# Storing and loading the second step's matrices in parts of 112 and 12 rows

## The chip, the core and the metric

The kernel runs on one core of a Trainium2 chip. The metric is the device time of one execution in microseconds. A core has TensorE (PE; its weight loads are listed as PEld), VectorE (DVE), ScalarE (ACT), GpSimd (POOL) and SyncE (SP). In this kernel all transfers between on-chip memory and DRAM are issued from SP's queue. They are carried out by 16 DMA engines.

## The reference

Two blocks follow one another. The first is a long convolution along the sequence, with a filter made by a small network, and the second a layer with a cosine gate:

```python
h_filt = (np.maximum(pos_emb @ w1, 0.0) @ w2) * np.exp(-0.01 * pos)[:, None]
u = x * v                                  # 4 x 12480 x 128
y = irfft(rfft(u, 2 * S) * rfft(h_filt, 2 * S)[None])[:, :S]
t = (x * y).reshape(4 * 12480, 128)
h = t @ moe_w_in                           # 128 x 2048
out = (h * np.cos(h)) @ moe_w_out          # 2048 x 128
```

All is float32.

## The kernel before

The convolution is done as a transform in two steps, as matrix products. The transform has N1 x N2 = 96 x 120 places. The first step (F1, `f1_units`) multiplies by a fixed matrix over the blocks. The second (F2) multiplies, for each of the 96 values k1, by a matrix w of its own, with KE = 124 rows and 120 columns. Then the result is multiplied with the filter's transform h, and two inverse steps (I1, I2) follow. There are four batches. In between, the rows that are ready go through the layer block ("moe"), 98 groups of 16 column blocks each.

The order of all work is written out by hand: `units` is a generator that makes one pass of a step for each `next`, and each engine carries out its own instructions in the order in which they were emitted. A pass j of a step has a `before` (loads or preparation, some passes ahead), an `mm` (matmuls) and an `after` (eviction and arithmetic, carried out during the next pass).

The second step exists in two forms, and each has 48 passes of two matrices.

- For batch 0 and the filter, `f2_both_units` runs alone on the core, with no layer work beside it. In `before`, `make_w` makes the two matrices of the next pass: ACT writes a scaled copy to PSUM (L328), and DVE adds the other term into the tile w (L330, three buffers). SP stores w to the DRAM tensor wd (L670). PE multiplies the filter's data (L490, or L493 in two halves) and the batch's data (L137). In `after`, ACT copies the filter's result into a tile h (L683, three buffers) and SP stores it to the DRAM tensor hd (L685). DVE makes two products with h (L506), and POOL combines them (L513). In the last pass a table cs is loaded as well (L672), which I1 uses.
- For batches 1 to 3, `f2_units` loads w from wd (L648) and h from hd (L650) two passes ahead, into three buffers each. It is interleaved with the layer's matmuls by the main loop.

Every row of a w tile is 960 bytes (two matrices of 120 numbers), and a row of an h tile is 2048 bytes with 120 rows.

After `f2_both_units` comes I1 (`i1_units`), whose matmuls need cs and the last results of L513. Then come I2 and, from about 300 us on, the layer.

Of the kernel before, what the change touches and what calls it, by code (L numbers as in the profile page):

```python
# [34 lines left out]
def kernel(  # L35
# [46 lines left out]
    nc = tc.nc  # L82
# [10 lines left out]
    KE = ODD + H  # L93
# [26 lines left out]
    wd = dram.tile([N1 // 2, KE, 2, N2], F32, name="wd")  # L120
# [192 lines left out]
    def last_tables(pool):  # L313
        rows = pool.tile([N1, 4, R], F32, name="rows")

        tw_t = pool.tile([N1, 2, N2], F32, name="tw_t")
        return rows, tw_t
# [18 lines left out]
    def make_w(w, k1, **how):  # L336


        turn(w, even[:, 0, :], even[:, 1, :], tw_w[:, 0, k1:k1 + 1], tw_w[:, 1, k1:k1 + 1],
             **how)  # L340
# [140 lines left out]
    def f2_mm(ps, w, k1, i, filt=False):  # L481


        k = k1 + i
        pi = ps[0:N2, :].rearrange("p (r b g i) -> p g r b i", r=2, g=2, i=2)[:, i]
        if not filt:
            mm(pi, w[:, i, :], parts[0:KE, :, k])
        elif k < KF:
            both = ftile[0:KE, :, k:k + N1 + 1:N1, :].rearrange("p b r i -> p r b i")
            nc.tensor.matmul(pi, w[:, i, :], both, start=True, stop=True)  # L490
        else:
            for r, src in enumerate((ftile[0:KE, :, k, :], above[0:KE, :, k - KF, :])):
                nc.tensor.matmul(pi[:, r], w[:, i, :], src, start=True, stop=True)  # L493

    def f2_product(pool, ps, h, k1, whole, engine=nc.gpsimd):


        y = parts[0:N2, :, k1:k1 + 2, :, :].rearrange("p r k b i -> p r b (k i)")
        t = pool.tile([N2, 2, CB, 4], F32, name="t", bufs=2)
        uu = ps[0:N2, :].rearrange("p (r b j) -> p r b j", r=2, j=4)  # L500
        if whole:
            for r, (dst, hh) in enumerate(((y, h[:, :, :, :]), (t[:, :, :, :], h[:, ::-1, :, :]))):
                u = uu[:, r]
                twice = bass.AP(tensor=u.tensor, offset=u.offset,
                                ap=[u.ap[0], [0, 2], *u.ap[1:]])
                nc.vector.tensor_tensor(dst, twice, hh, op=ALU.mult)  # L506
                yield
        for r, op in ((0, ALU.subtract), (1, ALU.add)):
            if not whole:
                nc.vector.tensor_tensor(y[:, r], uu[:, 0], h[:, r], op=ALU.mult)  # L510
                yield
                nc.vector.tensor_tensor(t[:, r], uu[:, 1], h[:, 1 - r], op=ALU.mult)  # L512
            (engine if r else nc.gpsimd).tensor_tensor(y[:, r], y[:, r], t[:, r], op=op)  # L513
            yield
# [59 lines left out]
    def units(n, steps, before, mm, after, parts, ahead=2, skip=0):  # L574


        for j in range(min(ahead, n)):
            for _ in before(j) or ():
                pass
        yield 0.0  # L580
        last = iter(())
        for j in range(n):
            early = iter(before(j + ahead) or () if j + ahead < n else ())
            now = None
            for i in range(parts):
                if i == skip or 2 * (i - skip) == max(parts, 2):
                    now = mm(j, now, int(i > skip))
                if i == 0 and parts == 1:
                    now = mm(j, now, 1)
                next(last, None)  # L590
                next(early, None)
                yield steps / parts
            for _ in early:
                pass
            next(last, None)
            last = after(j, now)
        for _ in last:
            pass
        yield REST
# [33 lines left out]
    def f1_units(bank, u, share, evict=f1_evict):  # L633
# [5 lines left out]

        return units(CB, F1_STEPS, lambda j: None, mm, lambda j, ps: evict(ps, j, share(j)), 2)  # L640

    def f2_units(bank):
        with tc.tile_pool(name="there", bufs=3) as pool:
            ws, hs = {}, {}

            def before(j):
                ws[j] = pool.tile([KE, 2, N2], F32, name="w")
                nc.sync.dma_start(ws[j][:, :, :], wd[j, :, :, :])  # L648
                hs[j] = pool.tile([N2, 2, CB, 4], F32, name="h")
                nc.sync.dma_start(hs[j][:, :, :, :], hd[j, :, :, :, :])  # L650

            def mm(j, ps, i):
                if i == 0:
                    ps = bank()
                f2_mm(ps, ws[j], 2 * j, i)
                return ps

            yield from units(N1 // 2, F2_STEPS, before, mm,
                             lambda j, ps: f2_product(pool, ps, hs.pop(j), 2 * j, False), 4)

    def f2_both_units(bank):

        with tc.tile_pool(name="both", bufs=2) as pool:
            ws = {}

            def before(j):
                ws[j] = pool.tile([KE, 2, N2], F32, name="w", bufs=3)
                for i in range(2):
                    make_w(ws[j][:, i, :], 2 * j + i, half=bank)
                nc.sync.dma_start(wd[j, :, :, :], ws[j][:, :, :])  # L670
                if j == N1 // 2 - 1:
                    nc.sync.dma_start(cs[:, :, :], csd[:, :, :])  # L672

            def mm(j, ps, i):
                if i == 0:
                    ps = bank(), bank()
                for k in range(2):
                    f2_mm(ps[1 - i], ws[j], 2 * j, k, filt=i == 0)
                return ps

            def after(j, ps):
                h = pool.tile([N2, 2, CB, 4], F32, name="h", bufs=3)
                nc.scalar.activation(h[:, :, :, :].rearrange("p r b j -> p (r b j)"),  # L683
                                     ps[1][0:N2, :], AF.Copy, scale=1.0 / M)
                nc.sync.dma_start(hd[j, :, :, :, :], h[:, :, :, :])  # L685
                last = j == N1 // 2 - 1
                yield from f2_product(pool, ps[0], h, 2 * j, not last,
                                      nc.vector if last else nc.gpsimd)

            yield from units(N1 // 2, F2_STEPS, before, mm, after, 4, ahead=1)  # L690
# [79 lines left out]
    def forward_units(bank, back):  # L770

        f2 = f2_units(bank)
        next(f2)
        yield from f1_units(bank, slots[0:R, :, :, :], lambda b: 1.0)
        yield from f2
        next(back)
        yield from i1_units(bank)
# [120 lines left out]
    with tc.manual_schedule():  # L898
        with tc.tile_pool(name="psum", bufs=8, space=PSUM) as psum, \
                ExitStack() as first:  # L900
            def bank():
                return psum.tile([P, BANK], F32, name="ps")
# [110 lines left out]
            rows, tw_t = last_tables(wpool)  # L1013
# [127 lines left out]
```

## Time and profile before

| what | value |
|---|---|
| median of three runs | 3636.73 us (3636.14 to 3637.93) |
| the profiled execution | 3637.09 us, of which its span is 3635.3 |
| granted TensorE clock, mean | 0.998 |
| PE busy | 3575.0 us (98%) |
| DVE busy | 2833.6 us (78%) |
| POOL busy | 2745.5 us (76%) |
| ACT busy | 2230.6 us (61%) |
| DMA, share of 16 engines (SP's queue) | 26.5%, 275 MB |
| stores of w (wd<-w) | 48 of 116.2 KB |
| loads of w (w<-wd) | 144 of 116.2 KB |
| stores of h, loads of h | 48 and 144 of 240 KB |

The profile records one execution. Its time is 1.8 us more than the span from the first to the last instruction. In lists of waits the numbers are the total in us, how many times, and the longest. In a timeline they are the start, the duration in us, and in brackets how long the engine was idle before and what ended that. In the tables by stretch of time each engine has its busy time and, in brackets, its number of instructions; behind them are the granted clock, the share of the DMA engines and GB/s. The rows of the DMA view that begin with "DMA" and digits cut the window into 40 slices and give the busy share of the 16 engines in tenths.

### The profile page before, as it was taken

Reading aid. Unit: us, or ns where it says so; the run is one execution under the profiler, and the core shown is the slowest. Engines: PE = TensorE matmul, PEld = TensorE weight load, DVE = VectorE, ACT = ScalarE, POOL = GpSimd, SP = SyncE. Lnnn points to the kernel's source line nnn. Section 1 sums busy time; section 2 is a strip of 40 time slices with the busy share of each in tenths; the row PEclk is TensorE's granted clock in tenths of the full one; section 3 lists DMA queues with packets and bytes.
Section 4 is the critical chain, followed back from the end, with each engine's and each line's share of the span. In section 5 each row is a group of like instructions: output and inputs, shape, how many; then the busy total and the mean of one; then the engine's idle time right before and its main releaser. Section 6 shows DMA issues by size and latency. Waiting matters only on the chain.

```text
span 3635.3 us, 101879 instructions
## 1 busy us (share of the span) xinstructions
PE 3575.0 (98%) x40826; PEld 2559.2 (70%) x40826; DVE 2833.6 (78%) x5289; ACT 2230.6 (61%) x4482; POOL 2745.5 (76%) x3237
## 2 busy tenths in 40 slices
PE   8999999999999999999999999999999999999999
PEld 7877767666678776666677776766667776666666
DVE  7877885688887886688887786578887667777877
ACT  7657666666554556656655556665655446666676
POOL 7767996688864896688864887588885558878777
PEclk9999999999999999999999999999999999999999
DMA  7444540022213550022211562022220350000000
GB/s 188 142 151 140 169 131 21 25 68 75 71 43 107 165 146 27 23 74 73 68 37 53 168 171 63 13 61 69 70 71 16 102 159 19 19 25 19 19 25 14
DMA packets 219584, 281.80 MB, mean 78 GB/s; under 512 B 18778, under 2 KB 156514, under 8 KB 218986
## 3 DMA queue, kind: packets, MB, share of 16 engines
q1 hardware_dynamic: 219114, 275.29, 26.5%
q8 instruction: 325, 5.32, 0.6%
q14 instruction: 145, 1.19, 0.1%
HBM read 194.75 MB, written 80.46 MB: 76 GB/s over the span
## 4 chain that ended last, share of the span: by engine, by line
PE 83%; DVE 5%; POOL 2%; ACT 1%; issue 1%; DMA 0%; SPq 0%; ACTq 0%; POOLq 0%; DVEq 0%
PE ph L137 30%; PE accb L846 17%; PE cv L137 17%; PE acca L846 13%; PE cv L457 3%; DVE gt L815 2%; DVE gt L821 2%; PE ph L141 1%; PE cv L141 1%; ACT gt L814 1%; POOL ts L829 1%; POOL slots L449 0%; POOL ts L832 0%; DVE t L512 0%; DVE slots L510 0%
## 5 line engine op out<-in xcount | busy, mean ns | idle before, releaser
L814 ACT ACTIVATE gt<-ph 128x512 int32<-128x512 f32 (+1 forms) x1380 | 821.9, 596 | 1083.5 <-PE ph L137 1029.0
L815 DVE SCALAR_TENSOR_TENSOR gt<-ph,gt 128x512 f32<-128x512 f32 (+1 forms) x1380 | 947.8, 687 | 666.1 <-ACT gt L814 661.9
L137 PE MATMUL ph<-at,w_in_sb 128*64 128x512 f32 (+1 forms) x5520 | 1432.0, 592 | 12.8 <-DVE gt L821 11.8
L829 POOL TENSOR_TENSOR ts<-gt 128x512 f32<-128x512 f32 (+2 forms) x784 | 998.9, 1274 | 569.7 <-PE accb L846 566.1
L820 ACT ACTIVATE gt<-gt 128x512 f32<-128x512 f32 (+1 forms) x1568 | 972.5, 620 | 5.9 <-DVE gt L815 4.7
L821 DVE TENSOR_TENSOR gt<-ph,gt 128x512 f32<-128x512 f32 (+1 forms) x1380 | 934.8, 677 | 0.0
L846 PE MATMUL accb<-ts,w_out_sb 128*64 128x128 f32 (+2 forms) x9408 | 653.4, 272 | 0.0
L832 POOL TENSOR_TENSOR ts<-ts,gt 128x256 f32<-128x256 f32 (+2 forms) x784 | 574.6, 733 | 61.5
L833 POOL TENSOR_TENSOR ts<-gt,ts 128x256 f32<-128x256 f32 (+2 forms) x784 | 573.5, 732 | 61.5
L846 PEld LDWEIGHTS acca<-gt,w_out_sb 128*64 128x64 f32 x6272 | 403.4, 136 | 256.3 <-issue 227.4
L846 PEld LDWEIGHTS accb<-ts,w_out_sb 128*64 128x64 f32 x9408 | 547.3, 137 | 0.0
L846 PE MATMUL acca<-gt,w_out_sb 128*64 128x128 f32 (+2 forms) x6272 | 481.9, 272 | 0.0
L846 PEld LDWEIGHTS accb<-gt,w_out_sb 128*64 128x64 f32 x3136 | 228.0, 136 | 245.4 <-issue 197.4
L137 PEld LDWEIGHTS ph<-at,w_in_sb 128*64 128x64 f32 x5520 | 360.1, 137 | 31.2 <-PE cv L141 11.3
L513 POOL TENSOR_TENSOR slots<-slots,t 120x256 f32<-120x256 f32 x383 | 277.5, 731 | 116.1 <-DVE t L512 63.0
L846 PE MATMUL accb<-gt,w_out_sb 128*64 128x128 f32 (+1 forms) x3136 | 314.3, 273 | 4.6 <-DVE ot L867 3.1
L846 PE MATMUL acca<-ts,w_out_sb 128*64 128x128 f32 (+1 forms) x3136 | 311.8, 272 | 2.6 <-POOL ts L832 2.3
L137 PEld LDWEIGHTS cv<-slots,tm 96*40 96x40 f32 (+1 forms) x3840 | 227.2, 125 | 121.4 <-issue 115.7
L137 PE MATMUL cv<-slots,tm 96*40 96x128 f32 (+1 forms) x3840 | 254.3, 273 | 4.3 <-DVE slots L535 3.4
L137 PEld LDWEIGHTS cv<-even,slots 120*64 120x64 f32 (+1 forms) x3072 | 168.3, 125 | 60.4 <-issue 58.2
L846 PEld LDWEIGHTS acca<-ts,w_out_sb 128*64 128x64 f32 x3136 | 204.4, 137 | 4.5 <-POOL ts L832 4.3
L137 PEld LDWEIGHTS cv<-slots,w 124*64 124x64 f32 (+1 forms) x1152 | 89.1, 134 | 154.1 <-issue 144.0
(136 smaller groups left out, 3875.2 us busy)
## 6 DMA issues: line engine op xcount, KB each, us to landing
h<-hd SPq DMA_DIRECT2D x144, 240.0 KB
tm<-td SPq DMA_DIRECT2D x96, 312.0 KB
xt<-in_x_dram SPq DMA_DIRECT2D x120, 208.0 KB
xs<-in_x_dram SPq DMA_DIRECT2D x120, 208.0 KB
zd<-xs SPq DMA_DIRECT2D x119, 208.0 KB
tile<-zd SPq DMA_DIRECT2D x96, 256.0 KB
vt<-in_v_dram SPq DMA_DIRECT2D x90, 208.0 KB
w<-wd SPq DMA_DIRECT2D x144, 116.2 KB
```

What stands on the lines that cost most here:

```text
L137: nc.tensor.matmul(dst[lo:hi], left[:, lo:hi], right, start=start, stop=stop)
L141: nc.tensor.transpose(dst, src, ident[0:n, 0:n])
L457: nc.tensor.matmul(dst[lo:hi], u[:, b, lo:hi, i], c1[0:u.shape[0], r:r + 2, :].rearrange("p r k -> p (r k)"), start=True, stop=True)
L513: (engine if r else nc.gpsimd).tensor_tensor(y[:, r], y[:, r], t[:, r], op=op)
L814: nc.scalar.activation(turns, ph[:, 0:m], AF.Identity, bias=phase)
L815: nc.vector.scalar_tensor_tensor(out=part, in0=ph[:, 0:m], scalar=phase, in1=turns, op0=ALU.add, op1=ALU.subtract)
L820: nc.scalar.activation(part, part, AF.Sin, scale=scale)
L821: nc.vector.tensor_tensor(part, ph, part, op=ALU.mult)
L829: nc.gpsimd.tensor_tensor(ts[:, 0:2, 0:half], gt[:, :, half:2 * half], gt[:, 0, 0:2 * half].rearrange("p (h n) -> p h n", h=2), op=ALU.sub ...
L832: nc.gpsimd.tensor_tensor(t[2], t[1], b11, op=ALU.add)
L833: nc.gpsimd.tensor_tensor(t[3], b21, t[2], op=ALU.subtract)
L846: nc.tensor.matmul(acc[h * CB:(h + 1) * CB, place, 0:r], w_out_sb[:, pair, weight, :], right[:, h * r:(h + 1) * r], start=(pair == 0 and i ...
```

## The change

A tuple of two slices cuts the 124 rows of w into the first 112 and the last 12. The store of w and the load of w are each issued as two transfers, one for each slice, to and from the same places. Nothing else differs: the same tiles and buffers, the same matmuls, the same order of everything else.

```diff
+    parted = slice(0, KE // 16 * 16), slice(KE // 16 * 16, KE)
+
     def f2_units(bank):
...
             def before(j):
                 ws[j] = pool.tile([KE, 2, N2], F32, name="w")
-                nc.sync.dma_start(ws[j][:, :, :], wd[j, :, :, :])
+                for rows in parted:
+                    nc.sync.dma_start(ws[j][rows, :, :], wd[j, rows, :, :])
                 hs[j] = pool.tile([N2, 2, CB, 4], F32, name="h")
                 nc.sync.dma_start(hs[j][:, :, :, :], hd[j, :, :, :, :])
...
                 for i in range(2):
                     make_w(ws[j][:, i, :], 2 * j + i, half=bank)
-                nc.sync.dma_start(wd[j, :, :, :], ws[j][:, :, :])
+                for rows in parted:
+                    nc.sync.dma_start(wd[j, rows, :, :], ws[j][rows, :, :])
                 if j == N1 // 2 - 1:
                     nc.sync.dma_start(cs[:, :, :], csd[:, :, :])
```

## The prediction

> **What bounds the kernel now.** I read the page first, then the windows, the waits and the timeline of the two stages that the diff touches, and last the DMA view of single transfers.
>
> ```profile
> span 3635.3 us, 101879 instructions
> PE 3575.0 (98%) x40826; PEld 2559.2 (70%) x40826; DVE 2833.6 (78%) x5289; ACT 2230.6 (61%) x4482; POOL 2745.5 (76%) x3237
> PE 83%; DVE 5%; POOL 2%; ACT 1%; issue 1%; DMA 0%; SPq 0%; ACTq 0%; POOLq 0%; DVEq 0%
> ```
>
> TensorE sets the end nearly everywhere and DMA has 0% of the chain. The chain is a share of the whole span, though. The stores of w lie in one stage, about 137 to 238 us; its waits say something else.
>
> ```profile
> ACT h L683 <- DMA hd<-h: 34.4, 41, 1.7
> DVE slots L506 <- ACT h L683: 12.5, 41, 1.1
> PEld ps L493 <- PE ps L137: 11.2, 22, 1.3
> ```
>
> 41 of the 48 passes wait for a store of h to land, because h has three buffers. DVE then waits for ACT, and PE for both. What that does to the pace is read from the starts of one kind of matmul; busy time does not show it, since the page models matmul ends.
>
> ```profile
> 141.43 1.03 PE L490 MATMUL ps<-ftile,w 124*120 124x256 f32 x4
> 143.17 1.03 PE L490 MATMUL ps<-ftile,w 124*120 124x256 f32 x4
> 144.67 0.60 ACT L683 ACTIVATE h<-ps 120x512 f32<-120x512 f32 x1 [1.04 <-DMA hd<-h]
> 144.90 1.03 PE L490 MATMUL ps<-ftile,w 124*120 124x256 f32 x4
> ...
> 201.09 0.60 ACT L683 ACTIVATE h<-ps 120x512 f32<-120x512 f32 x1 [0.74 <-DMA hd<-h]
> 203.11 0.60 ACT L683 ACTIVATE h<-ps 120x512 f32<-120x512 f32 x1 [0.74 <-DMA hd<-h]
> 205.13 0.60 ACT L683 ACTIVATE h<-ps 120x512 f32<-120x512 f32 x1 [0.74 <-DMA hd<-h]
> ```
>
> Until the first wait a pass takes 1.735 us (141.43 to 144.90 is two passes), PE back to back. Afterwards it takes 2.02. From the pass at 139.70 to the last at 232.77 there are 46 passes: 93.1 us, mean 2.023.
>
> Why does the store of h land late? The first DMA line and packet count below are of a window with one load of w alone (710.4 to 716 us), the second count of one load of 128 rows alone (570.8 to 575), the third of the store stage (137 to 238).
>
> ```profile
> DMA  0000000290200022222220000000000000000000
> DMA packets 128, 0.12 MB, mean 21 GB/s; under 512 B 4, under 2 KB 128, under 8 KB 128
> DMA packets 145, 0.28 MB, mean 66 GB/s; under 512 B 16, under 2 KB 16, under 8 KB 144
> DMA packets 12666, 17.57 MB, mean 174 GB/s; under 512 B 911, under 2 KB 6983, under 8 KB 12656
> ```
>
> A load of w is 124 packets of a row and 4 small ones, and keeps 2 tenths of the 16 engines busy for 1.3 us: four engines carry it, 31 rows each. The transfer of 128 rows closes with 16 small packets. In the store stage 48 x (4 + 15) = 912 fit the 911: w on 4 engines, h on 15. The trace's completion records say the same and give the pattern for other row counts: 96 and 128 rows 16 engines, 120 rows 15, 104 rows 13, 124 rows 4, always the largest divisor up to 16. They also show the store of h issued at 201.85: eleven completions by 3.23 us after issue, the last four at 4.67 to 5.24. Single packets take 44 ns (960 B row of w) and 84 ns (2048 B row of h) in the median, so a pass loads the shared four engines with 31 x 44 + 8 x 84 = 2.04 us. That is the 2.02 us period. These four engines bound the stage.
>
> **The change, part by part.**
>
> *Stores.* 112 rows should go to 16 engines (7 rows each) and 12 rows to 12 (one each), an estimate from the divisor pattern above. The fullest engine then has 8 x 44 + 8 x 84 = 1.02 us a pass; with the mean packet times of the stage (47 and 119 ns) 1.33. Both lie under 1.735, so this bound goes. What is late next:
> - PE needs 1.735 a pass.
> - DVE: starts at 199.70, 200.31, 200.91 and two w products 0.25 apart, 1.71; its new wait for a second store may add one more 21 ns wait instruction of L330, 1.73.
> - The loop through the three h buffers: ACT 0.60, the wait for SP 0.2 plus 0.4 for the new issue ahead of it, landing 3.2 plus 8 x 0.047 for the added rows, over three passes: 4.8 / 3 = 1.6.
> - SP: w issues cost 0.24 us (4 engines) and transfers on 13 to 16 engines 0.31 to 0.38, so 0.35 + 0.31 + 0.37 = 1.03.
>
> PE and DVE are within 0.03 of each other, and PSUM banks couple them; I take 1.75, bounds 1.735 and 1.85. Gain 46 x (2.023 - 1.75) = 12.6 us, bounds 13.3 and 8.0.
>
> *End of the stage.* The last data matmuls start at 233.75 and the next step at 238.48, released by POOL. In these 4.73 us ACT waits for h twice more. Without that DVE does the two products of pass 46 in 1.21 us, and POOL's three L513 follow as now (236.08 to 238.48, 2.40). That is 3.61, a gain of 1.1. The load of cs sits behind one more issue on SP (0.35 us); its completions on the free engines came 2.1 us after issue, so it stays ahead.
>
> *Clock.* The PE gap there shrinks from 3.71 to 2.6 us.
>
> ```profile
> 243.00:244.00 1.00, 1.00 (x7) 1.00 (x7) 0.14 (x1) 0.32 (x1) 0.00 (x0) 0.50 1.02 418
> 245.00:246.00 1.00, 1.00 (x12) 1.00 (x11) 0.00 (x0) 0.67 (x2) 0.35 (x1) 1.00 0.96 343
> 548.00:550.00 2.00, 1.02 (x5) 0.63 (x7) 0.59 (x1) 0.00 (x0) 1.92 (x4) 0.60 0.00 0
> ```
>
> The seventh column is granted clock: 0.50 until 244.62 (the trace's clock records: 6.83 us from 237.79), which costs the matmuls from 238.48 on 3.07 us. After a gap of 2.35 us (546.63 to 548.98) it also fell, for 3.41 us. So a gap of 2.6 may cost nothing, one such stretch (1.7) or the same as now. I take a gain of 1.3, bounds 0 and 3.1. The Trainium skill ("TensorE: Matmul & The Clock Gate", Part 1: The HAM clock gate) has the clock drop after at least one idle window of about 3.4 us; by it 2.6 us would cost nothing and the sum would be 1.8 us lower. The drop at 548.40 came after 1.77 us of idle, so here the trace is harsher than the rule.
>
> *Loads.* 144 loads become 288. No wait for w shows in those three passes, the DMA share there is 0.15 to 0.27, and a load is issued two passes ahead. SP gets 144 x 0.35 us more, in stretches in which it mostly waits for buffers; queued behind it are the h loads, the loads of the layer's tiles and output stores. PE must wait for one more completion per pass: at most 144 x 51 ns (the wait instructions of L137 there) = 7.3 us, if matmuls do not cover it. They do now: at 705.26 and 705.37 two of them run while matmuls from 705.25 to 706.29 are under way. I take 0 and keep 7.3 for the range. A gain is excluded, as nothing waits for these loads.
>
> Sum against the profiled execution: 3637.1 - 12.6 - 1.1 - 1.3 = 3622.1. The median is 0.4 lower, so 3621.7. All that follows the stage is PE-bound and moves forward with it. A comparison of this kernel can tell about 0.2%, 7.3 us.
>
> **Rivals.**
>
> *A. The parts share one limit.* If the write path as a whole held the stage at its 171 to 186 GB/s, spreading rows would change nothing: 3637. For it: the rate is steady over 90 us. Against it: with h alone in the queue 234 to 235 us shows 251 GB/s, and eleven of fifteen completions are early. The Trainium skill ("DMA: Bandwidth & Descriptors", Rules for kernel authors) speaks for A: two transfers to disjoint partitions go one after the other on the same engines, so one should not bother. It supposes that the undivided transfer sprays over all 16; this one has 4. Chance 0.05.
>
> *B. The parts are not spread*, 28 and 3 rows on the same four engines: the same 31 x 44 ns, 3637. Against it: the divisor pattern over five row counts. 0.03.
>
> *C. Another loop steps in at once*, such as the h loop or the banks, with a period near 1.90: 46 x 0.12 + 1.1 = 6.6 us, 3630. For it: landing would need 4.1 us instead of 3.6. 0.05.
>
> *D. Slower: SP becomes the bound.* Three issues a pass decide once they average more than 2.02 / 3 = 0.67 us. A full queue stretches an issue: that of h at 145.62 took 1.13. At 0.75 each a pass takes 2.25, 46 x 0.23 = 10.6 us longer, 3647. Against it: the median of h is 0.378, and those stretched stand where the four engines were backlogged. 0.05.
>
> **How the numbers follow.** My forecast has the remaining 0.82, at 3621.7. Its own range runs from 3617 (1.735 a pass, no clock loss there, and none at 548, where the drop costs half of 548.98 to 551.82, 1.4: 18.9 us in all) to 3630 (1.80 a pass, no clock gain and half of the 7.3). That holds C as well and leaves out A, B, D and the outermost corners. Faster by over 0.2%: 0.82 and a little of C, 0.84. Within 0.2%: A, B, the rest of C and the corner where every PE wait counts, 0.11. Slower: D, 0.05.
>
> **What would show it.** Right: no ACT wait for hd<-h after the first passes, L490 and L493 starts 1.74 to 1.8 us apart, the i1 matmuls starting near 225 us, and 48 x (16 + 12 + 15) small packets in the store stage. Wrong: a period still near 2.02 (A, B), SP issues of w above 0.6 us (D), ACT still waiting for hd<-h at about 1.9 (C), or PE gaps ahead of the first w matmuls from 705 us on.

## The result and the profile after

The changed kernel takes 3617.86 us in the median of six runs (3617.44 to 3621.77), the kernel before 3636.13 (3633.47 to 3637.93). The ratio is 0.9953, with an interval of 0.994 to 0.9966: 17 us less by the ratio, 18 by the medians. The profiled execution after took 3621.77 us (span 3620.0), 15.3 less than the one before. It is the longest of the six, and why comes out below.

The page of after, its first lines:

```profile
span 3620.0 us, 102190 instructions
PE 3565.4 (98%) x40826; PEld 2560.2 (71%) x40826; DVE 2830.0 (78%) x5289; ACT 2228.6 (62%) x4482; POOL 2749.6 (76%) x3237
```

The same matmuls, fewer busy microseconds, and the same 98%: the share says nothing about what was won. The waits of the store stage do (137 to 224 us of after; the lines of `f2_both_units` have moved by 4, so L683 is L687):

```profile
ACT h L687 <- PE ps L493: 11.6, 20, 0.6
ACT h L687 <- PE ps L490: 11.3, 19, 0.6
...
ACT h L687 <- DMA hd<-h: 4.3, 5, 1.4
```

Of 41 waits for a store of h five are left, 4.3 us instead of 34.4. The prediction had expected none after the first passes; these are later. Each follows an issue on SP that took unusually long: a store of h issued at 170.33 took 1.81 us, and ACT waited at 174.37, 175.98 and 177.40; parts of w issued at 204.62 and 218.52 took 0.98 and 1.06 us, and ACT waited at 207.12 and 221.12. Otherwise ACT now waits for PE, which is the other way round from before. The timeline of after shows the pace from the start of the stage and late in it:

```profile
139.66 1.03 PE L490 MATMUL ps<-ftile,w 124*120 124x256 f32 x4
141.39 1.03 PE L490 MATMUL ps<-ftile,w 124*120 124x256 f32 x4
143.13 1.03 PE L490 MATMUL ps<-ftile,w 124*120 124x256 f32 x4
144.86 1.03 PE L490 MATMUL ps<-ftile,w 124*120 124x256 f32 x4
...
201.22 0.74 SPq L674 DMA_DIRECT2D wd<-w  x2
201.66 0.60 ACT L687 ACTIVATE h<-ps 120x512 f32<-120x512 f32 x1 [0.61 <-PE ps L493]
202.06 0.32 SPq L689 DMA_DIRECT2D hd<-h  x1
...
203.41 0.60 ACT L687 ACTIVATE h<-ps 120x512 f32<-120x512 f32 x1 [0.61 <-PE ps L493]
```

The 1.735 us of the first passes now lasts; from 201.66 to 203.41 a pass takes 1.75. From ACT's sixth h to its 41st the mean is 1.744 us, against 2.048 before. PE waits for nobody between 140 and 219 us. DVE has hardly more room, as the stretch 175 to 185 us shows, before and after (PE, PEld, DVE, ACT and POOL in this order):

```profile
175.00:185.00 10.00, 9.79 (x59) 7.44 (x58) 8.84 (x21) 6.14 (x16) 6.95 (x10) 1.00 0.63 186
```

```profile
175.00:185.00 10.00, 10.00 (x70) 9.13 (x70) 10.00 (x24) 6.99 (x20) 7.90 (x13) 1.00 0.78 228
```

The DMA view of 137 to 224 us counts the small packets that close each engine's share:

```profile
DMA packets 13899, 17.72 MB, mean 204 GB/s; under 512 B 2070, under 2 KB 8142, under 8 KB 13889
```

48 x (16 + 12 + 15) = 2064, and the load of cs closes with up to 15 more. So 112 rows went to 16 engines and 12 rows to 12. The completion records (the times at which each engine reports its share of a transfer as landed) of after put the part issued at 201.22 at 1.64 to 2.06 us after its issue, the small part at 1.48 to 1.79, and the store of h issued at 202.06 at 2.05 to 2.47, with no late group of four.

### The profile page after: what moved, and what is told of

Same layout as the page of the kernel before. It is cut to its first block, busy times and chain, and to the rows that moved or that the text cites. A ratio compares the mean times of both kernels' runs of the same rounds, so it can differ in the third digit from the quotient of the medians.

```text
span 3620.0 us, 102190 instructions
## 1 busy us (share of the span) xinstructions
PE 3565.4 (98%) x40826; PEld 2560.2 (71%) x40826; DVE 2830.0 (78%) x5289; ACT 2228.6 (62%) x4482; POOL 2749.6 (76%) x3237
## 4 chain that ended last, share of the span: by engine, by line
PE 83%; DVE 5%; POOL 2%; ACT 1%; issue 1%; DMA 0%; ACTq 0%; POOLq 0%; DVEq 0%; SPq 0%
PE ph L137 30%; PE accb L850 17%; PE cv L137 17%; PE acca L850 13%; PE cv L457 3%; DVE gt L825 2%; DVE gt L819 2%; PE ph L141 1%; PE cv L141 1%; POOL ts L833 1%; ACT gt L818 1%; POOL slots L449 0%; POOL ts L836 0%; DVE t L512 0%; DVE slots L510 0%
## 5 line engine op out<-in xcount | busy, mean ns | idle before, releaser
L137 PE MATMUL ph<-at,w_in_sb 128*64 128x512 f32 (+1 forms) x5520 | 1432.9, 592 | 12.9 <-DVE gt L825 11.9
L137 PEld LDWEIGHTS ph<-at,w_in_sb 128*64 128x64 f32 x5520 | 359.9, 137 | 31.4 <-PE cv L141 11.3
L137 PEld LDWEIGHTS cv<-slots,tm 96*40 96x40 f32 (+1 forms) x3840 | 227.7, 125 | 120.7 <-issue 116.0
L137 PE MATMUL cv<-slots,tm 96*40 96x128 f32 (+1 forms) x3840 | 254.5, 273 | 4.1 <-DVE slots L535 3.4
L137 PEld LDWEIGHTS cv<-even,slots 120*64 120x64 f32 (+1 forms) x3072 | 167.8, 125 | 61.1 <-issue 57.8
L137 PEld LDWEIGHTS cv<-slots,w 124*56 124x56 f32 (+1 forms) x1152 | 89.1, 134 | 154.1 <-issue 143.9
```

The lines of the kernel that those rows point to most:

```text
L137: nc.tensor.matmul(dst[lo:hi], left[:, lo:hi], right, start=start, stop=stop)
```

## The experiments

Theory T is that of the prediction: four engines carried all of w and bounded the store stage, and nothing waited for the loads. The rivals were that the loads count (L), that PE's added waits cost time (W), that the write path as a whole is the limit (A), that smaller parts help whatever their rows (P), and that SP's issues become the bound (D).

**Only the stores, and only the loads.** The first kernel leaves the load in `f2_units` whole, the second leaves the store in `f2_both_units` whole:

```diff
 # stores alone: in f2_units
-                for rows in parted:
-                    nc.sync.dma_start(ws[j][rows, :, :], wd[j, rows, :, :])
+                nc.sync.dma_start(ws[j][:, :, :], wd[j, :, :, :])
 # loads alone: in f2_both_units
-                for rows in parted:
-                    nc.sync.dma_start(wd[j, rows, :, :], ws[j][rows, :, :])
+                nc.sync.dma_start(wd[j, :, :, :], ws[j][:, :, :])
```

> Only the stores of w are issued in parts of 112 and 12 rows; the loads stay whole. Theory T (the four engines that carry w bound the store stage, and nothing waits for the loads): the whole gain is here, about 3618 us, with the passes of the store stage 1.735 us apart and the i1 matmuls starting near 224 us. Rival L (a good part of the gain comes from the loads in the three later passes, which leave four engines free for other transfers): 3625 or more. Rival W (the second completion that PE waits for in each load costs time): below 3618, down to 3611.

> Only the loads of w are issued in parts; the stores stay whole. Theory T: no change, 3636 us within 2 us, the store stage with its 2.02 us a pass. Rival L: faster by several us. Rival W: slower by up to 7 us (144 x 51 ns).

Stores alone: 3616.53 us (3616.15 to 3621.18), ratio 0.9952 (0.9939 to 0.9964), all of the gain. Loads alone: 3634.29, ratio 0.9999 (0.999 to 1.0008), none. The waits of the kernel with only the loads in parts, 137 to 238 us:

```profile
ACT h L686 <- DMA hd<-h: 36.0, 43, 1.7
```

The old wait is all there. Of L and W the interval leaves room for no more than 0.1%, 3.6 us. The added PE waits exist: over the same piece of work (705.3 to 1015.3 us before, 690 to 1000 after) the wait instructions of L137 grow from 141 to 176. PE's busy time does not, 305.89 and 305.90 of 310 us. Matmuls cover them in this stretch.

**Smaller parts on fewer engines.** Against the kernel with only the stores in parts:

```diff
-    parted = slice(0, KE // 16 * 16), slice(KE // 16 * 16, KE)
+    parted = slice(0, KE // 2), slice(KE // 2, KE)
```

> The stores of w are issued in two parts of 62 rows each; loads whole. Both parts are smaller than the whole, but by the divisor pattern 62 rows go to 2 engines each. Theory T: the two fullest engines carry 62 x 44 + 8 x 84 ns = 3.4 us a pass, so the store stage grows by 46 x (3.4 - 2.02) = 63 us against the kernel before, to about 3700 us. Rival A (the write path as a whole is the limit, the rows' place on engines does not matter): 3636. Rival P (two smaller transfers help whatever their rows): 3618.

Measured 3699.38 us (3698.95 to 3701.21), ratio 1.0176 (1.016 to 1.0191): 64 us slower than the kernel before, where T had said 63. The sum hit so closely in part by luck: in the profiled executions the 46 passes took 59.6 us more, since the first of them still ran faster, and 4.4 us came from the end of the stage, which the sum had left out. The DMA view and the waits, 137 to 300 us:

```profile
DMA packets 12676, 17.60 MB, mean 108 GB/s; under 512 B 907, under 2 KB 6975, under 8 KB 12666
```

```profile
ACT h L686 <- DMA hd<-h: 105.2, 45, 3.9
```

48 x (2 + 2 + 15) = 912 small packets fit the 907: each 62 rows went to two engines. The same bytes as before move at 108 GB/s instead of 174, and a pass takes 3.413 us, where 62 x 44 + 8 x 84 ns is 3.40. The completion records of the store of h issued at 200.67 have 13 engines at 3.58 us or sooner and the last two at 8.05 and 8.10. P and A cannot give this.

**One part, with a row count that divides well.** The tiles are made 128 rows high, and four computed rows are stored and loaded that no matmul uses:

```diff
-    wd = dram.tile([N1 // 2, KE, 2, N2], F32, name="wd")
+    wd = dram.tile([N1 // 2, P, 2, N2], F32, name="wd")
-    even = const.tile([KE, 2, N2], F32, name="even")
+    even = const.tile([P, 2, N2], F32, name="even")
...
-            mm(pi, w[:, i, :], parts[0:KE, :, k])
+            mm(pi, w[0:KE, i, :], parts[0:KE, :, k])
```

> The tiles w and wd get 128 rows (four more rows are computed, stored and loaded, and never used by a matmul); each store and load is one transfer of 128 rows, 120 KB. Theory T: 128 rows go to 16 engines, 8 rows each, so the fullest engine has 8 x 44 + 8 x 84 ns as with 112 and 12, and the time is that of the changed kernel, 3618 us within 2, although there is one transfer again and 3% more bytes. Rival P (the gain needs two parts): 3636.

3619.12 us (3616.03 to 3619.98), ratio 0.9954 (0.9941 to 0.9966). The DMA view from 137 to 224 us:

```profile
DMA packets 13533, 17.92 MB, mean 206 GB/s; under 512 B 1502, under 2 KB 7766, under 8 KB 13523
```

The 1502 small packets are 48 x (16 + 15) + 15 less one. One transfer with more bytes does as well as two: the spread over engines is what counts, not the parting.

**Five parts.** With the engines loaded as in the change, again against the kernel with only the stores in parts:

```diff
-    parted = slice(0, KE // 16 * 16), slice(KE // 16 * 16, KE)
+    parted = [slice(r, r + 32) for r in (0, 32, 64)] + [slice(96, 112), slice(112, KE)]
```

> The stores of w are issued in five parts of 32, 32, 32, 16 and 12 rows (16, 16, 16, 16 and 12 engines), so the load of the engines stays that of 112 and 12 rows; loads whole. SP then issues six transfers in a pass. Rival D put the point from which SP decides at the issues of a pass adding up to more than the pass. At the 0.31 to 0.38 us of the page's issues, 5 x 0.34 + 0.37 = 2.1 us a pass, so 46 x (2.1 - 1.735) = 17 us more than with two parts: about 3634 us, with SP issuing without a break. If SP's issue is free beside everything else: 3617. If stretched issues of 0.75 us are the rule with many in flight: 4.1 us a pass, 3720.

3667.83 us (3667.59 to 3668.16), ratio 1.0091 (1.0077 to 1.0105): SP decides, as D says, but far more than expected. SP's own waits in 137 to 225 us come first, and then its issues of two passes from the timeline:

```profile
SPq L688 <- ACT h L686: 1.5, 4, 0.5
SPq L673 <- DVE w L330: 1.5, 1, 1.5
SPq L688 <- ACT ps L328: 0.3, 1, 0.3
```

```profile
201.49 2.92 SPq L673 DMA_DIRECT2D wd<-w  x5
204.50 0.32 SPq L688 DMA_DIRECT2D hd<-h  x1
204.92 2.15 SPq L673 DMA_DIRECT2D wd<-w  x5
207.17 0.32 SPq L688 DMA_DIRECT2D hd<-h  x1
```

SP hardly waits for anyone. Five issues of w take 2.15 us, or 2.92 where one of them is stretched (the trace has it at 1.17), and h another 0.42 with the step to the next. A pass without a stretched issue is 2.67 us (204.50 to 207.17), and the mean from the sixth to the 41st is 2.782. The expectation took the duration of an issue, 0.34; here issues that follow one another start 0.39 to 0.49 apart. That is most of the miss, and the stretched issues are the rest.

**Each w stored twice**, the second time to a tensor of its own, on top of the kernel with 128 rows:

```diff
                 nc.sync.dma_start(wd[j, :, :, :], ws[j][:, :, :])
+                nc.sync.dma_start(wd2[j, :, :, :], ws[j][:, :, :])
```

> As the kernel with one part of 128 rows, and each w is stored a second time to a tensor of its own that nobody reads; so 236 KB more... in all 480 KB leave the chip's memory in a pass, in transfers of 16 and 15 engines. Theory T: the fullest engine has 16 x 44 + 8 x 84 ns = 1.38 us a pass in the median and 16 x 47 + 8 x 119 = 1.70 by the mean packet times, both under 1.735: no change, 3619 within 3. Rival A (the write path as a whole is limited to the 186 GB/s of the kernel before): 480 KB would need 2.6 us a pass, 46 x 0.9 = 41 us more, 3660.

3625.01 us (3624.05 to 3629.59), ratio 0.9974 (0.9965 to 0.9984). The stretch 175 to 185 us and a wait of 137 to 228:

```profile
175.00:185.00 10.00, 10.00 (x70) 9.17 (x69) 9.69 (x23) 6.03 (x17) 7.73 (x12) 1.00 0.89 273
```

```profile
ACT h L685 <- DMA hd<-h: 26.2, 34, 2.1
```

273 GB/s go out with a third more bytes in a pass, so A falls: 186 GB/s was no limit of the path. T's "within 3" is missed by 3: from ACT's sixth h to its 41st a pass takes 1.831 us, and the wait for h is back, at 89% of all engines. Against the kernel with one part of 128 rows, the 46 passes take 2.5 us more and the end of the stage 2.0 us more. The mean packet times (1.70 us a pass) were the better estimate than the median (1.38), and even they were too low this near to the bound.

**The scatter.** Executions of one and the same kernel lay between 3616 and 3622. The matmul gaps behind the store stage and ahead of batch 1 were filled with matmuls whose results are not used, on top of the kernel with only the stores in parts. The second gap gets five of them, and two in a second version:

```diff
             yield from units(N1 // 2, F2_STEPS, before, mm, after, 4, ahead=1)
+            spare = bank()
+            for _ in range(8):
+                nc.tensor.matmul(spare[0:N2, 0:2 * CB], ws[N1 // 2 - 1][:, 0, :],
+                                 ftile[0:KE, :, 0, :], start=True, stop=True)
...
                         tc.tile_pool(name="ps_c", bufs=3, space=PSUM))
+                    spare = bank()
+                    for _ in range(5):
+                        nc.tensor.matmul(spare[:, :], w_in_sb[:, 0:P], w_in_sb[:, 0:BANK],
+                                         start=True, stop=True)
```

> As the kernel with only the stores in parts, and PE gets matmuls whose results are not used in two gaps: 8 of 128 columns behind the last pass of the store stage (1.75 us of the gap of 1.92) and 5 of 512 columns ahead of the first step of batch 1 (2.15 us of the gap of 2.35). Theory K (each of these gaps costs up to 1.7 us by a stretch of 3.41 us at clock 0.50, in some executions and not in others): the granted clock stays 1.00 from 12 us to the last 10, and the executions lie together at the low end of those without the filling, 3616 us, where the kernel without it scatters from 3616 to 3622. If the clock has nothing to do with that scatter: the same scatter as without. If the filling is too long: some tenths of a us slower.

> The kernel with only the stores in parts once more, on the chip and in the call of the filled one, to compare the two. Theory T: 3616 to 3622 as before. Theory K: the profiled execution's time is the higher, the more stretches at clock 0.50 follow the gaps at 220 and 527 us, by 1.7 us each.

> As the filled kernel, with the second filling cut from 5 to 2 matmuls of 512 columns: each took 0.86 us there (two records of 0.43), so 5 took 4.3 us where the gap was 2.35, and the first step of batch 1 started 2.4 us late. Two take 1.7. Theory K: clock 1.00 throughout and 1.7 us less than the kernel without filling for each stretch at 0.50 that it had; no later start of the first step of batch 1. All executions within 3614 to 3618, the 1.4 us that the executions differ by ahead of the store stage included. Otherwise the same times as without filling, 3616 to 3622.

> The kernel with only the stores in parts, beside the newly filled one on the same chip: 3616 to 3622, with 0, 1 or 2 stretches at clock 0.50 in the profiled execution.

With 8 and 5 matmuls: 3618.92 us (3618.59 to 3620.46), beside 3620.99 (3617.50 to 3622.27) without. The second filling was too long:

```profile
527.67 4.56 PE L1064 MATMUL cv<-w_in_sb 128*128 128x512 f32 x10
...
532.16 0.55 PE L457 MATMUL cv<-c,slots 104*64 104x192 f32 x4
```

With 8 and 2: 3617.40 (3616.47 to 3618.14), beside 3619.21 (3617.06 to 3623.28) without. This is as fast as the changed kernel (ratio to the kernel before 0.9953, 0.994 to 0.9967). The medians with and without filling do not differ by more than can be told, but the spread is 1.7 us instead of 6 (1.9 instead of 4.8 in the first pair). The profiled executions show where it comes from. The first column of times is from the first i1 matmul to the first of the layer, the second from the first step of batch 1 to its second step:

| profiled execution | us | stretches at clock 0.50 behind the two gaps | i1 to layer | F1 to F2 |
|---|---|---|---|---|
| changed kernel | 3621.77 | 3.41 and 3.41 us | 60.62 | 157.81 |
| stores in parts, second time | 3621.62 | 3.41 and 3.41 | 60.62 | 157.79 |
| stores in parts, third time | 3621.03 | 3.41 and 3.41 | 60.61 | 157.82 |
| one part of 128 | 3619.51 | 3.41 and none | 60.62 | 156.11 |
| stores in parts, first time | 3616.15 | none | 58.96 | 156.13 |
| filled, 8 and 2 | 3616.47 | none | 58.96 | 156.13 |

Each stretch costs 1.7 us, in its place and in no other. The third number from the end of these lines is the granted clock, and the count behind PE's busy time says how many matmuls ran; they are the stretch 224 to 227 us of the changed kernel and, below it, of the kernel with only the stores in parts the first time:

```profile
224.00:227.00 3.00, 3.00 (x17) 3.00 (x17) 0.72 (x2) 0.37 (x2) 0.50 (x2) 0.50 0.43 107
```

```profile
224.00:227.00 3.00, 3.00 (x31) 3.00 (x31) 1.93 (x6) 1.62 (x4) 0.59 (x1) 1.00 0.86 286
```

The gap was the same 1.92 us in both. What differs is where it lies. In all twelve traces every change of the granted clock comes a whole multiple of 3.413 us after the first one: in the changed kernel from 12.39 to 224.02 us it is 62 of them. Cut each trace into windows of 3.413 us on that grid and add up PE's idle time in each, leaving out the last 25 us. The clock fell at the end of all 17 windows that began at full clock and held 1.87 us of idle or more, and of none that held 1.62 or less. (The ends of matmuls are modelled, so these limits are rough.) In the changed kernel the whole gap of 1.92 us lay in one window (220.60 to 224.02). In the kernel with only the stores in parts, the first time, a boundary at 221.32 cut it into 1.11 and 0.81 us.

Up to 1.9 us of scatter lie ahead of the store stage: the first product of w starts between 135.8 and 137.7 us in all these kernels, changed or not. That goes with the place of the grid too. The clock first reaches 1.00 at 9.5 to 12.9 us, and over the twelve traces the start of the first product follows it, by some 0.56 us for each us.

The filling is therefore less proven than it looks. In both filled kernels that were profiled the clock first reached 1.00 early (9.95 and 10.56 us), and by an estimate from the grid a boundary would have cut the first gap even without the filling: the gap begins 84.3 us behind the first product of w, and the boundaries lie at 221.6 and 222.2 us, so at most 1.4 us of it would have lain in one window. For the filling speak the recorded mean clocks: 1.000 in all five executions with 8 and 5 matmuls, and beside them, without filling, 0.999 in the three above 3620 us and 1.000 in the two below 3618.

## Why the prediction was right

The forecast was 3621.7, the median 3617.9, and the profiled execution moved by 15.3 us where the sum had 15.0. That these two agree so closely is partly luck: the terms measured 12.9, 1.8 and 1.2, and 0.7 was lost again between the first and second step of batch 1 (157.81 us against 157.13, with one stretch at clock 0.50 in both). The median lies at the low end of the range, whose outermost terms add up to 3617.8. The mechanism held; from execution to execution the total also moves with the clock. Term by term, from the two profiled executions:

- *The bound before.* 31 x 44 + 8 x 84 ns as the period: shown by taking it both ways, 1.74 us a pass with the load spread, 3.41 with two engines.
- *The pass after.* Predicted 1.75, measured 1.74: from the pass at 139.66 to the last at 219.79 it is 80.1 us for 46 passes, 12.9 less than before (predicted 12.6). PE is the next bound, back to back from the first pass, and DVE is close behind it: where it does not wait, its own pass is 1.70 us (176.70, 178.40, 180.10), where the prediction had 1.71 to 1.73.
- *The end of the stage.* Predicted 1.1, measured 1.8: from the last data matmuls to i1 it is 2.94 us instead of 4.73. The sum had let DVE begin the products of pass 46 when those matmuls start; their first half was done by then, because the last passes have no w left to make. The sum also let both waits of ACT for h go, and one stayed: 1.40 us, ending at 221.12.
- *The clock.* Predicted 1.3, chosen between three outcomes. In the profiled execution the stretch fell from 6.83 to 3.41 us and gave 1.2 back (61.85 to 60.62). In four of the six runs the total is 3.8 us lower in the mean than in the other two. Fewer stretches (1.7 us each) and an earlier start of the store stage (up to 1.9) can make that difference, and with it the distance from 3621.7 to the median. How many stretches these four had is not known, since the trace kept is that of the longest; their mean clock is 0.999, as in all six. Behind the gap of 1.92 us four of the five profiled executions of the table that were not filled had a stretch at 0.50, and one had none. The rule of the Trainium skill ("TensorE: Matmul & The Clock Gate", Part 1: The HAM clock gate), that the clock drops after a whole idle window, would have allowed none of the four; the measurements decide, and the rule is too mild here. What fits all twelve traces is the idle time within one window of the grid above: 1.92 us in the four, 1.11 in the one. This is read from traces after the fact; no run moved a gap on purpose.
- *The loads.* Predicted 0, measured 0 within 0.1%.
- *SP.* The three issues of a pass came to 0.74 + 0.32 = 1.06 us against 1.03. D is real as a mechanism, but at the spacing of the kernel with five parts (1.735 - 0.42) / 0.45 = 2.9 issues of w fit into a pass, and the change has two, which start 0.36 us apart. That a full queue stretches an issue, as D supposed, is not shown: the stretched issues of the changed kernel lie in stretches of 10 us in which the engines were busy to 0.71 to 0.75.
- *The rule against parting.* "DMA: Bandwidth & Descriptors", Rules for kernel authors, of the Trainium skill advises against two transfers for disjoint partitions. For a transfer that uses all engines the experiments do not contradict it: one part of 128 rows did as well. For 124 rows, which used four, parting was worth 17 us.

## What to carry to other kernels

Look at how many engines a transfer uses before its size: count its closing small packets in a window that holds it alone, or compare its GB/s with that of a neighbour, and choose row counts with a large divisor up to 16 (pad, or part off the remainder). It pays only where a wait for a transfer sets the pace, so take the pace from the starts of one repeated instruction, not from busy time or from shares of the whole span. Part into few pieces: in a row of six each issue costs SP some 0.45 us, and six of them to a pass of 1.74 us made this stage slower than it had been.

## What the runs showed that was not expected

An issue on SP lasts 0.31 to 0.42 us by its record. Two in a row start 0.36 us apart in the changed kernel, six in a row 0.39 to 0.49 apart in the kernel with five parts. Now and then one is stretched to between 1.0 and 1.8 us with the engines not full on average, and in the changed kernel the waits that are left follow such issues. What stretches them stays open.

The granted clock falls to 0.50 behind a PE gap of 1.92 us in some executions and not in others, for 3.41 us each time. As far as the twelve traces show, it falls where most of the gap lies in one window of a grid of 3.413 us, and the place of that grid differs from execution to execution. A gap of under two microseconds can so cost 1.7 more than its own length, and one kernel's executions can lie 6 us apart (3617.06 and 3623.28): compare many of them.
